# When a gate's product may start: a time for one transposing transfer in the list of an attention and mixture-of-experts kernel

## The chip, the cores and the metric

The kernel runs on one core of one Trainium2 chip. The metric is the device time of one execution in microseconds, the median of several runs. The core's engines are named as the profile names them: PE (TensorE) multiplies, and PEld is its loading of weights; DVE (VectorE) and ACT (ScalarE) work on elements and empty PSUM; POOL (GpSimd) works on elements in SBUF and issues gathers; SP (SyncE) issues nearly all other transfers. Each engine works through its own list of instructions in order, and the lists wait for each other by semaphores.

## The reference

Two stages follow each other. The first is causal attention with a decay, over 8 batches of 8 heads with 576 positions of 64 elements. The second routes every token to one of 8 experts, and each token's expert can depend on the token before it:

```python
decay = cum[:, :, :, None] - cum[:, :, None, :]          # cum: cumsum of log f
scores = np.where(causal, -1e9, scale * q @ k.T + decay)
attn = softmax(scores);  x = attn @ v                    # x: [8, 576, 512]
logits = x @ w_gate                                      # 512 -> 8
local_gate = sigmoid(x @ w_local)
for b, s:  e = argmax(logits[b, s]) if s == 0 or local_gate[b, s] < 0.5 else prev_e
           out[b, s] = softmax(logits[b, s])[e] * (relu(x[b, s] @ w1[e]) @ w2[e])
```

## The kernel before

Attention runs batch by batch, from 0 to 7. A batch is cut into 25 units. A unit has steps on several engines: scores on PE into a PSUM bank `st` (`sc`), a maximum `nm` on DVE (`mx`), the exponential `P` on ACT (`ex`), its transposes on PE into `pt` (`tr`), the high half `ph` on ACT (`hi`), the low half `pl` on DVE (`lo`), and the product with v on PE into `xp` (`av`). Numbers are carried as a high and a low half in 16 bits, so products come in threes. Twenty units treat the 512 first queries of a batch, the last five the 64 last queries, whose result is `xnl`.

Beside its own units a batch carries the preparation of the next one: POOL splits the loaded `ldq`, `ldk` and `ldv` into halves (`t16q`, `t16k`, `VH`, `VL`), PE transposes them into `st`, ACT or DVE copies them out as `Aq` and `Ak`, and SP copies parts of these into `QB` and `KB`. `pump` hands these steps out, some before each unit, from `queue`.

When a batch is done, its result goes the same way: POOL splits `xn` into `xr` and `xnl` into `xl`; SP transposes `xr` in two transfers into `xt` (`turn_x` in `finish_main`) and `xl` in one into `xlt` (`turn_x` in `finish_last`, L781), and writes both to DRAM as `xs`. A batch later, `gate(b)` multiplies them by the gate's weights on PE: its step `mult` (L804) is 32 products of `xt` and 8 of `xlt` into one PSUM bank, `half` and `add` bring the logits together in `L`. Every second gate is followed by the steps of `route`, which find each token's expert and its place; the largest of them is `marks` (L1475), five long instructions, on DVE for the third group of two batches, partly on POOL for the first two.

The order of all these is written by a planner while the kernel is built. It keeps a clock for every engine (`clock`, in modelled nanoseconds), a list of steps for each stage (`line`) and one list, `chain`, for gates and routing. `issue` (L1221) asks `start_of` for each stage and `side_next` (L1184) for the chain when the next step could start, takes the one whose time plus a weight is smallest, and emits it. A chain's step that is possible at once has the weight -700, so it goes first; one that isn't has the weight 0. A gate enters the chain after the unit `GI` of the next batch (unit 21, 14 or 12). `side_next` holds `mult` back until `XD` says that all three transposing transfers of its batch have been emitted (`XD` is 3); for the time it takes those to be done the planner has no number. The seven gates from 0 to 6 go through this chain; that of batch 7 is placed by hand behind attention, as is the whole expert stage, whose first steps begin while attention ends: the gathers `xg` of the first experts' tokens, and the splitting of expert 0's weights on POOL (`stg` into `wh`, `wl`, `uh`, `ul`).

Of the kernel before, what the change touches and what calls it, by code (L numbers as in the profile page):

```python
# [63 lines left out]

T0 = 9700.0
DUE = (("k2", 11000), ("q2", 12500), ("k3", 14500), ("q3", 15500), ("v", 18000), ("v4", 20500), ("a", 26000), ("b", 29000))

NB = (4, 5, 4)
NOV = 31
# [3 lines left out]
def kernel(  # L73
# [208 lines left out]
    def split(hi, lo, t, fast):  # L282
        if fast:
            nc.scalar.copy(hi, t)
            nc.vector.tensor_tensor(lo, t, hi, ALU.subtract)
        else:
            nc.gpsimd.tensor_scalar(hi, t, 1.0, 1.0, ALU.mult, ALU.mult)
            nc.gpsimd.tensor_tensor(lo, t, hi, ALU.subtract)
# [16 lines left out]
    def hi_lo(hi, lo, t, n):  # L305

        m, w = t.shape[1], 1
        for d in t.shape[2:]:
            w *= d
        out = [(m * w, lambda: nc.gpsimd.tensor_scalar(hi, t, 1.0, 1.0, ALU.mult, ALU.mult))]  # L310
        for i in range(0, m, n):
            e = min(i + n, m)
            out.append((2 * (e - i) * w,
                        lambda i=i, e=e: nc.gpsimd.tensor_tensor(lo[:, i:e], t[:, i:e], hi[:, i:e], ALU.subtract)))
        return out
# [421 lines left out]
        clock["DVE"] += 600  # L737


    XT, XD = {}, {}  # L740

    def finish_main(b, xn):
        xr = pools["small"].tile([128, 4, 2, DM], F16, name="xr", bufs=1)
# [30 lines left out]
    def finish_last(b, xnl):  # L774
        xl = pools["small"].tile([128, 2, 4, 64], F16, name="xl", bufs=1)
        xlt = pools["small"].tile([128, 4, 128], F16, name="xlt", bufs=1)
        XT[b].append(xlt)
        t0 = b * S + 512

        def turn_x():  # L780
            nc.sync.dma_start_transpose(out=xlt, in_=xl.rearrange("p a j d -> p (a j d)"))  # L781
            put_xl()
            XD[b] = XD.get(b, 0) + 1

        def put_xl():
            for r in range(2):
                nc.sync.dma_start(out=xs[t0:t0 + 64].rearrange("q (a r e) -> r q a e", a=2, r=2)[r],
                                  in_=xl[r * 64:(r + 1) * 64].rearrange("q a j d -> q a (j d)"))

        if b == B - 1:  # L790
            split(xl[:, 0], xl[:, 1], xnl, True)
            EX["xl"] = xl, xlt
            put_xl()
        else:
            for i, x in enumerate(hi_lo(xl[:, 0], xl[:, 1], xnl, 4) + [(0, turn_x)]):
                queue.insert(min(XI, len(queue)) + i, x)
# [37 lines left out]
    def compute(b, T):  # L834
# [268 lines left out]
        for j in range(4):  # L1103
            d1unit(j)
        d2unit()
        then(-1, lambda: finish_last(b, X["xnl"]))
        lb, lc = (max((i for i in range(20) if i % 5 == x), key=UO.index) for x in (3, 4))
        if b < B - 1:
# [27 lines left out]
    clock = {"PE": T0, "ACT": T0, "DVE": T0, "POOL": T0}  # L1136
# [36 lines left out]
    POOL = 1  # L1173
    OPENS = "mult", "rows", "ends", "carries", "back", "place", "invert", "pinvert", "fill"
    SHUTS = "add", "rows2", "hold", "scan1", "onehot", "place2", "invert2", "pinvert2", "fill2"
    chain = deque()
    side = {"end": (0.0, "PE"), "run": None, "cost": None}
# [6 lines left out]
    def side_next():  # L1184
        eng, cost = COSTS.get(chain[0].__name__, ("DVE", 160))
        after = [side["end"]]
        if chain[0] is early_tok and "open" not in EX or XD.get(getattr(chain[0], "batch", None), 0) < 3 and hasattr(chain[0], "batch"):
            return None, eng, cost
        if chain[0].__name__ in OPENS and side["run"] is None:
            if not room["psS"]:  # L1190
                return None, eng, cost
            after.append(min(room["psS"]))
        now = 0 if side["cost"] is POOL else clock[eng]
        return max([now] + [t + WAIT[src, eng] for t, src in after]), eng, side["cost"] or cost

# [25 lines left out]
    def issue(until=None):  # L1221
        while any(line.values()):
            ready = [(start_of(st), line[st][0][0] + RANK[st], st) for st in STAGES if line[st]]
            if chain:
                ready.append((side_next()[0], serial[0] + RANK["side"], "side"))
                W["side"] = side_weight(*side_next())
            t, _, st = min((x for x in ready if x[0] is not None), key=lambda x: (x[0] + W[x[2]], x[1]))
            if due and due[0][0] <= t and all(room[r] for r in due[0][2]):
                due.popleft()[1]()
                continue  # L1230
            if st == "side":
                side_issue(*side_next())
                continue
            n, u, prev = line[st].popleft()
            eng, cost, fn, takes, frees = u[st]
            for r, c in takes.items():
                for _ in range(c):
                    room[r].remove(min(room[r]))
            fn()
            clock[eng] = t + cost  # L1240
            ends[n, st] = t + cost, eng
            if st == "eq":
                turned[u["key"]] = t + cost
            for r, c in frees.items():
                room[r] += [ends[n, st]] * c
            if (n, st) == until:
                return
# [493 lines left out]
    def open_small():  # L1741
# [7 lines left out]
          "a": due_a, "b": due_b, "nop": nop}  # L1749
    due.extend((T, DO[f], ("psS", "psT") if f in ("k2", "k3", "q2", "q3") else ()) for f, T in DUE)  # L1750

# [515 lines left out]
```

## Time and profile before

| what | value |
|---|---|
| time, median of 3 runs | 856.01 us (855.11 to 859.09) |
| the profiled execution's own time | 858.83 us |
| its span | 857.1 us, 21126 instructions |
| PE busy | 785.4 us, 92% of the span |
| DVE, ACT, POOL busy | 62%, 51%, 48% of the span |
| mean granted clock of PE | 0.976 of full |

The span is what the profiler saw between the first and the last instruction; the execution's own time is 1.7 us more. Attention fills the time from the start to 431 us, the experts the rest.

### The profile page before, as it was taken

The page shows a single profiled execution, that of the slowest core. Times are in us where ns is not written, and L with a number is a line of the kernel's source. Part 1 is how long each engine was busy: PE and PEld are TensorE (multiplying, and loading weights), DVE is VectorE, ACT ScalarE, POOL GpSimd, SP SyncE. Part 2 cuts the span into 40 slices and gives each one's busy share as a digit, 9 for nine tenths or more (in the row PEclk, how much of TensorE's full clock was granted, in tenths as well). Part 3 has the DMA queues.
Part 4 walks back from the last instruction along what each step waited for, and adds up shares of the span by engine and source line. Part 5 has one row for each costly group of instructions (what it writes and reads, how often), then busy time and mean ns, then how long its engine had stood idle before and what let it go on. Part 6 is the DMA issues. An engine that isn't in the chain of part 4 may idle for free. (4 is left out here: it accounts for less than half of the span.)

```text
span 857.1 us, 21126 instructions
## 1 busy us (share of the span) xinstructions
PE 785.4 (92%) x8510; PEld 546.9 (64%) x8510; DVE 529.3 (62%) x1125; ACT 434.4 (51%) x807; POOL 408.9 (48%) x479
## 2 busy tenths in 40 slices
PE   5897999889998799878987899999999999999996
PEld 3676778767877678767753555575564847566543
DVE  8885878898867888798848742443163644525120
ACT  4785878758866688657821413333242423324221
POOL 9598938488753968532976252221311212130201
PEclk9998999999989999998999999999999999999999
DMA  7979768596781859329674641848264553736101
GB/s 167 192 165 193 160 112 168 123 180 144 140 197 42 157 140 158 70 47 229 161 165 185 194 142 50 216 147 203 95 171 149 155 182 121 193 116 185 51 0 47
DMA packets 196517, 122.46 MB, mean 143 GB/s; under 512 B 136220, under 2 KB 172318, under 8 KB 196396
## 3 DMA queue, kind: packets, MB, share of 16 engines
q1 hardware_dynamic: 190273, 101.68, 51.6%
q0 software_dynamic: 6144, 19.41, 7.0%
q8 instruction: 68, 1.11, 0.5%
q14 instruction: 32, 0.26, 0.1%
HBM read 72.41 MB, written 19.62 MB: 107 GB/s over the span
## 5 line engine op out<-in xcount | busy, mean ns | idle before, releaser
L1690 PE MATMUL z<-xT,wh 128*128 128x288 f16 (+4 forms) x960 | 182.3, 301 | 3.8 <-DVE hl L1671 3.8
L899 ACT ACTIVATE P<-st,nm 128x512 f32<-128x512 f32 (+3 forms) x288 | 152.4, 584 | 38.5 <-DVE nm L879 35.3
L879 DVE TENSOR_REDUCE nm<-st 128x1 f32<-128x512 f32 (+4 forms) x264 | 134.1, 542 | 23.2 <-PE st L875 16.8
L1671 DVE SCALAR_TENSOR_TENSOR hl<-z,hh 128x576 f16<-128x576 f32 (+5 forms) x80 | 53.0, 662 | 154.0 <-ACT hh L1670 153.8
L919 ACT CAST ph<-pt 128x512 f16<-128x512 f32 (+1 forms) x200 | 115.8, 583 | 50.1 <-PE pt L914 48.6
L914 PE MATMUL pt<-ident,P 128*128 128x128 f32 x784 | 124.7, 283 | 13.0 <-DVE pl L923 8.0
L923 DVE TENSOR_TENSOR pl<-pt,ph 128x512 f16<-128x512 f32 x168 | 111.6, 668 | 26.3 <-ACT ph L919 24.0
L1690 PEld LDWEIGHTS <-wh 128*128 128x128 f16 x960 | 93.2, 98 | 43.7 <-issue 4.9
L1690 PE MATMUL z<-xT,wl 128*128 128x288 f16 (+4 forms) x480 | 118.4, 301 | 0.0
L1712 PE MATMUL y<-uh,hh 128*128 128x512 f16 x288 | 109.9, 381 | 1.6 <-ACT o L1680 1.6
L1712 PE MATMUL y<-uh,hl 128*128 128x512 f16 x288 | 109.9, 382 | 0.0
L1712 PE MATMUL y<-ul,hh 128*128 128x512 f16 x288 | 109.7, 381 | 0.0
L1670 ACT ACTIVATE hh<-z 128x576 f16<-128x576 f32 (+5 forms) x80 | 46.0, 575 | 121.1 <-PE z L1690 121.0
L914 PEld LDWEIGHTS pt<-ident,P 128*128 128x128 f32 x784 | 85.8, 144 | 28.9 <-issue 7.5
L1712 PEld LDWEIGHTS <-hh 128*128 128x128 f16 x576 | 56.5, 98 | 70.4 <-issue 6.2
L1682 POOL DMA_INDIRECT out_dram<-o,ranki x26 | 27.3, 1051 | 149.0 <-ACT o L1680 115.8
L893 PE MATMUL xp<-VH,pl 128*128 128x65 f16 (+1 forms) x960 | 92.3, 195 | 4.3 <-DVE pl L923 4.3
L893 PE MATMUL xp<-VH,ph 128*128 128x65 f16 (+1 forms) x960 | 94.3, 198 | 0.9 <-ACT ph L919 0.9
L893 PE MATMUL xp<-VL,ph 128*128 128x65 f16 (+1 forms) x960 | 93.2, 196 | 0.0
L893 PEld LDWEIGHTS <-ph 128*128 128x128 f16 (+1 forms) x1920 | 85.0, 103 | 7.7 <-issue 2.5
L868 PE MATMUL st<-KB,QB 70*128 70x256 f16 (+4 forms) x448 | 80.1, 287 | 8.5 <-DMA KB<-Ak 7.1
L868 PE MATMUL st<-Ak,Aq 128*128 128x256 f16 (+4 forms) x448 | 80.7, 291 | 7.3 <-ACT P L899 7.1
(390 smaller groups left out, 1316.3 us busy)
## 6 DMA issues: line engine op xcount, KB each, us to landing
stg<-in_moe_w_dram SPq DMA_DIRECT2D x64, 512.0 KB
xs<-xr SPq DMA_DIRECT2D x16, 512.0 KB
ldq<-in_q_dram SPq DMA_DIRECT2D x14, 512.0 KB
ldk<-in_k_dram SPq DMA_DIRECT2D x14, 512.0 KB
ldv<-in_v_dram SPq DMA_DIRECT2D x28, 256.0 KB
QB<-Aq SPq DMA_DIRECT2D x15, 256.0 KB
KB<-Ak SPq DMA_DIRECT2D x15, 256.0 KB
ldv<-in_v_dram SPq DMA_DIRECT2D x20, 64.0 KB
```

Of the source, the lines that this page charges most:

```text
L868: nc.tensor.matmul(st[p0:p0 + m, co:co + n], lhsT=queries(lq, kk, h, c), rhs=rhs, start=(ps == 0 and first and co == col), stop=(ps == 1), ...
L879: nc.vector.tensor_reduce(dst, src, axis=AX.X, op=ALU.max, negate=True)
L893: nc.tensor.matmul(xo, lhsT=a[:, c0:c0 + m], rhs=w[:, vi, :], start=False, stop=(i == n - 1 and jj == 2), skip_group_check=True)
L899: nc.scalar.activation(P[:, c0:c1].rearrange("p (k x r) -> p k r x", r=2, x=64), st[:, c0:c1].rearrange("p (k r x) -> p k r x", r=2, x=64) ...
L914: nc.tensor.matmul(U["pt"][:, i * 128:(i + 1) * 128], lhsT=P[:, i * 128:(i + 1) * 128], rhs=ident, is_transpose=True, start=(i == 0), stop ...
L919: nc.scalar.copy(U["ph"][:, :cols], U["pt"][:, :cols])
L923: nc.vector.tensor_tensor(U["pl"][:, :cols], U["pt"][:, :cols], U["ph"][:, :cols], ALU.subtract)
L1670: nc.scalar.activation(hv, z[:, 0:nh, 0:wd], AF.Relu)
L1671: nc.vector.scalar_tensor_tensor(lv, z[:, 0:nh, 0:wd], 0.0, hv, ALU.max, ALU.subtract)
L1682: nc.gpsimd.indirect_dma_start(out=outf, out_offset=bass.IndirectOffsetOnAxis(ap=scat(t), axis=0), in_=o, in_offset=None, bounds_check=NT ...
L1690: nc.tensor.matmul(z[:, a, 0:wd], lhsT=w[:, d, fc * 128:(fc + 1) * 128], rhs=xT[:, x, a * wd:(a + 1) * wd], start=(i == 0), stop=(i == len ...
L1712: nc.tensor.matmul(y, lhsT=a[:, fc, t * 128:(t + 1) * 128], rhs=u[:, fc], start=(i == 0), stop=(i == len(prods) - 1))
```

## The change

A number `XL` is added, and `finish_last` notes, when it emits the transposing transfer of a batch's `xl`, a time `XR`: the later of POOL's and PE's modelled clocks at that moment plus 4500 modelled nanoseconds. `side_next` then lets no gate's first step start in the plan before that time. The emitted instructions are the same in kind and number on each engine; their order is not.

```diff
 DUE = (("k2", 11000), ("q2", 12500), ...
+XL = 4500
...
-    XT, XD = {}, {}
+    XT, XD, XR = {}, {}, {}
...
             nc.sync.dma_start_transpose(out=xlt, in_=xl.rearrange("p a j d -> p (a j d)"))
             put_xl()
             XD[b] = XD.get(b, 0) + 1
+            XR[b] = max(clock["POOL"], clock["PE"]) + XL
...
             after.append(min(room["psS"]))
+        if hasattr(chain[0], "batch") and side["run"] is None:
+            after.append((XR[chain[0].batch], "PE"))
         now = 0 if side["cost"] is POOL else clock[eng]
```

Lines behind the change are up to four further down in the new kernel: L816 is L818 there, L868 is L870, L781 is L782, L1479 is L1483.

All five lists are the same up to gate 3, so gates 0, 1 and 2 stand where they stood. On PE, gate 3 follows the products with v at once in the kernel before:

```order
5760 L893 MATMUL xp<-VL_126,ph 128x65
5761 L893 LDWEIGHTS pl
5762 L893 MATMUL xp<-VH_124,pl 128x65
5763 L816 LDWEIGHTS xt
5764 L816 MATMUL st<-wg,xt 128x18
```

In the new kernel attention's own work follows there:

```order
5761 L895 LDWEIGHTS pl
5762 L895 MATMUL xp<-VH_124,pl 128x65
5763 L870 LDWEIGHTS Aq
5764 L870 MATMUL st<-Ak,Aq 128x512
5765 L870 LDWEIGHTS QB_120
5766 L870 MATMUL st<-KB_122,QB_120 128x512
5767 L877 LDWEIGHTS mA
5768 L877 MATMUL st<-mB,mA 128x128
5769 L916 MATMUL pt<-ident,P 128x128 x4
```

and gate 3 begins in row 5928 (100 matmuls further down):

```order
5925 L895 MATMUL xp<-VL_126,ph 128x65
5926 L895 LDWEIGHTS pl
5927 L895 MATMUL xp<-VH_124,pl 128x65
5928 L818 LDWEIGHTS xt
5929 L818 MATMUL st<-wg,xt 128x18
```

So only gate 3 itself is moved back in this place. Behind it, everything that the planner decides comes out otherwise: gate 4 begins in row 7130 (row 7192 before), gate 5 in row 8335 (row 8374 before), gate 6 in row 9514 (row 9492 before). On SP, the transposing transfer for gate 5 stood behind the copies into `QB_121` and the parts of `KB_123`:

```order
162 L351 DMA QB_121<-augt 3x512
163 L757 DMA xs<-xr 64x4x1024 x2
164 L378 DMA QB_121<-Aq 64x2x1024 x2
165 L382 DMA QB_121<-Aq 64x512
166 L339 DMA KB_123<-augm 3x4096
167 L351 DMA KB_123<-augt 3x512
168 L781 DMA_TRANSPOSE xlt<-xl 128x4x128
```

and now stands ahead of them:

```order
161 L352 DMA QB_121<-augt 3x512
162 L758 DMA xs<-xr 64x4x1024
163 L782 DMA_TRANSPOSE xlt<-xl 128x4x128
164 L789 DMA xs<-xl 128x1x256 x2
165 L758 DMA xs<-xr 64x4x1024
166 L379 DMA QB_121<-Aq 64x2x1024 x2
167 L383 DMA QB_121<-Aq 64x512
```

The transfer for gate 5 no longer waits in SP's list for those copies. The steps of `route` move too. On DVE, the five instructions of the third `marks` (from `HI` to `LO`) followed each other without a step of attention between them, just as batch 7 begins:

```order
592 L1473 TENSOR_TENSOR hm<-t_192,ov 128x10
593 L1479 TENSOR_TENSOR HI<-imain,hm 128x480
594 L1483 TENSOR_SCALAR RH<-HI,irow 128x10x48
595 L1485 TENSOR_SCALAR RH<-HI,irow 128x2x48
596 L1490 TENSOR_TENSOR RH<-HI,icol 128x10x48
597 L1491 TENSOR_TENSOR LO<-i_176,lo 128x1280
598 L879 TENSOR_REDUCE nm<-st 128x1 x5
```

and now stand among low halves `pl` of batch 6's last units:

```order
590 L1483 TENSOR_TENSOR HI<-imain,hm 128x480
591 L925 TENSOR_TENSOR pl<-pt,ph 128x512
592 L1487 TENSOR_SCALAR RH<-HI,irow 128x10x48
593 L925 TENSOR_TENSOR pl<-pt,ph 128x512
594 L1489 TENSOR_SCALAR RH<-HI,irow 128x2x48
595 L925 TENSOR_TENSOR pl<-pt,ph 128x256
596 L1494 TENSOR_TENSOR RH<-HI,icol 128x10x48
597 L1495 TENSOR_TENSOR LO<-i_176,lo 128x1280
598 L956 RECIPROCAL rs<-xp 128x4
599 L881 TENSOR_REDUCE nm<-st 128x1
```

Only the last two of the five stand side by side now, and the third `marks` comes before batch 6's last units are done, no longer after. Two smaller moves go with these. The second `marks`, in batch 5, begins in row 441 on DVE (row 422 before). And on POOL the first three quarters of the splitting of expert 0's first weights (`stg`, `wh`, half of `wl`) stand ahead of the six gathers `xg` instead of behind them.

## Rows read from the trace of the kernel before

**Rows 1.** The page: busy time by engine, granted clock in 40 slices.
```profile
PE 785.4 (92%) x8510; PEld 546.9 (64%) x8510; DVE 529.3 (62%) x1125; ACT 434.4 (51%) x807; POOL 408.9 (48%) x479
PEclk9998999999989999998999999999999999999999
```
**Rows 2.** Waits of PE, whole span: us in total, times, longest.
```profile
PE st L868 <- ACT P L899: 7.1, 6, 4.7
PE st L816 <- DMA xlt<-xl: 4.4, 2, 2.4
```
**Rows 3.** Timeline of PE at gate 3: start, us, instruction, idle time before.
```profile
243.86 0.95 PE L816 MATMUL st<-wg,xt 128*128 128x18 f16 x32
246.74 0.59 PE L816 MATMUL st<-wg,xlt 128*64 128x18 f16 x8 [1.94 <-DMA xlt<-xl]
247.27 1.12 PE L914 MATMUL pt<-ident,P 128*128 128x128 f32 x4
```
**Rows 4.** Timeline of PE at gate 5.
```profile
347.88 0.95 PE L816 MATMUL st<-wg,xt 128*128 128x18 f16 x32
351.26 0.42 PE L816 MATMUL st<-wg,xlt 128*64 128x18 f16 x8 [2.42 <-DMA xlt<-xl]
352.11 0.65 PE L914 MATMUL pt<-ident,P 128*128 128x128 f32 x4
```
**Rows 5.** Timeline of SP at gates 3, 4 and 5.
```profile
243.77 1.83 SPq L781 DMA_TRANSPOSE xlt<-xl  x1
...
282.32 2.29 SPq L781 DMA_TRANSPOSE xlt<-xl  x1
...
348.76 1.23 SPq L781 DMA_TRANSPOSE xlt<-xl  x1
```
**Rows 6.** Timeline of POOL: the split that gate 3's transfer waits for.
```profile
237.41 0.67 POOL L314 TENSOR_TENSOR xl<-xnl,xl 128x256 f16<-128x256 f32 x1
```
**Rows 7.** Line L816 at gate 4: count, duration ns, first and last start.
```profile
L816 PE MATMUL st<-wg,xlt x8: 177/177/198, 309.4 to 309.7; 128*64 128x18 f16 x8
```
**Rows 8.** Windows behind both waits: engines' busy time, instructions, clock, DMA, GB/s.
```profile
246.70:253.50 6.80, 6.76 (x42) 5.35 (x43) 3.34 (x11) 2.65 (x6) 0.58 (x2) 0.50 0.90 219
352.30:355.90 3.60, 3.60 (x30) 2.61 (x29) 2.99 (x10) 1.61 (x4) 3.35 (x6) 0.53 0.02 5
```
**Rows 9.** Line L974, once per batch: first and last mark used here.
```profile
L974 PE MATMUL st<-mB,mA x4: 193/193/203, 106.6 to 106.7; 128*128 128x64 f16 x4
...
L974 PE MATMUL st<-mB,mA x4: 193/193/203, 360.7 to 360.8; 128*128 128x64 f16 x4
```
**Rows 10.** Windows from mark to mark, batches with gates 1, 3 and 5.
```profile
106.60:152.30 45.70, 43.80 (x752) 36.59 (x746) 37.17 (x90) 36.95 (x78) 27.01 (x27) 1.00 0.74 148
206.90:256.40 49.50, 47.38 (x740) 38.82 (x739) 38.07 (x90) 37.35 (x77) 31.63 (x32) 0.93 0.73 154
311.70:360.70 49.00, 46.02 (x747) 37.65 (x739) 38.56 (x93) 37.69 (x77) 33.64 (x35) 0.97 0.60 113
```
**Rows 11.** Window ahead of gate 3.
```profile
203.60:243.80 40.20, 40.02 (x688) 32.99 (x685) 32.91 (x74) 33.05 (x67) 30.96 (x32) 1.00 0.72 147
```
**Rows 12.** Timeline of DVE: first and last of the third marks' five.
```profile
380.89 1.46 DVE L1479 TENSOR_TENSOR HI<-imain,hm 128x480 f16<-128x480 f16 x1
...
385.05 1.48 DVE L1491 TENSOR_TENSOR LO<-i,lo 128x1280 f16<-128x1280 f16 x1
```
**Rows 13.** Timeline of PE there.
```profile
387.92 0.59 PE L868 MATMUL st<-Ak,Aq 128*128 128x512 f16 x1 [4.66 <-ACT P L899]
```
**Rows 14.** Window behind it.
```profile
386.80:393.30 6.50, 5.38 (x29) 3.87 (x28) 4.43 (x11) 4.52 (x10) 0.00 (x0) 0.50 1.08 256
```
**Rows 15.** Timeline of POOL: first gather, last low half of expert 0's first weights.
```profile
395.26 1.24 POOL L1643 DMA_INDIRECT xg<-xs,xg  x1 [10.74 <-DVE pl L923]
...
424.52 2.27 POOL L314 TENSOR_TENSOR wl<-stg,wh 128x512 f16<-128x512 f32 x2
```
**Rows 16.** Timeline of PE: the first expert's first products.
```profile
431.16 0.50 PE L1690 MATMUL z<-xT,wh 128*128 128x384 f16 x2
```

## The prediction

> **What bounds the kernel now.** I read the page first. PE is busy 92% of the span, the next engine 62% [rows 1], so what PE stands idle for is what can be won, and the row of the granted clock shows a second thing to win: it is not at full level everywhere [rows 1]. Next came PE's waits, longest in total first. Among them one belongs to the change: the gate's products wait for the transfer into `xlt` twice, 4.4 us in all [rows 2]. The timeline shows where. At gate 3 the 32 products of `xt` are done by 244.8 us and the first of `xlt` starts at 246.74, 1.94 us of idle time before it [rows 3]. At gate 5 it is the same with 2.42 us, up to 351.26 [rows 4]. The other gates from 0 to 6 do not wait for it: the wait's count is two, and both are seen.
>
> The windows behind the waits show that PE loses more than the idle time. From 246.7 to 253.5 the granted clock is 0.50, so 1.2 instead of 2.4 GHz, and PE is busy 6.76 of these 6.8 us; from 352.3 to 355.9 it is 0.53 with PE busy throughout [rows 8]. Ahead of gate 3 the clock was 1.00 for 40.2 us with PE busy 40.02 of them [rows 11], so the fall follows the wait. Four transposes take 1.12 us at the lower level and 0.65 at the higher [rows 3, 4].
>
> **Why the transfers come late.** POOL finishes the split of `xl` for gate 3 at 238.1 [rows 6], but SP issues the transfer only at 243.77 [rows 5], after the copies and parts that stand ahead of it in its list. PE comes to the gate at 243.86 [rows 3]: issue and use coincide, and the data is there 2.9 us after the issue (246.7 less 243.8). Gate 5 has 348.76 and 347.88 [rows 4, 5]. Gate 4's transfer, which stands ahead of those copies, is issued at 282.32 [rows 5] and first used at 309.4 [rows 7], with no wait.
>
> **The change, part by part.**
>
> *The new time itself.* It adds no instruction and no wait on the chip; it moves rows in the lists. Up to gate 3 nothing moves, so some 244 us are as before.
>
> *Gate 3* goes behind 100 further matmuls. Ahead of the gate PE did 688 in 40.2 us [rows 11], 58 ns each, so it reaches the gate 5.8 us later, at 249.7, and `xlt` after 0.95 us of `xt` products, at 250.6. The data landed at 246.7, and the lists of SP and POOL up to its transfer are the same, so the margin is 3.9 us. The wait goes, and what stands in its place is attention's scores, which read the same `Aq`, `Ak`, `QB` and `KB` as the scores just before. What is late next there is nothing that the trace shows, as the margin is larger than the wait.
>
> *Gate 5* comes 20 matmuls earlier, 1.2 us, but its transfer goes to the place in SP's list that gate 4's transfer had in the kernel before: in front of the copies. Gate 4's was issued 27 us ahead of use [rows 5, 7], so this wait goes as well. What is queued behind the transfer on SP are the copies into `QB_121` and `KB_123`; they need data that POOL splits after `xl`, so they lose about the transfer's 1.23 us of issuing [rows 5] and no more. They are needed when batch 7 begins, some 20 us later.
>
> *Gates 4 and 6* move by 31 matmuls forward and 11 back, 1.8 and 0.6 us at 58 ns. Gate 4 keeps over 20 of its 27 us. Both cost nothing.
>
> *What the two waits are worth.* The first bound is the idle time alone, 1.94 + 2.42 = 4.4 us. The second adds half of PE's busy time at the lower level, 3.4 + 1.8, and makes 9.6; but PE would then run into the other engines sooner. Between the bounds lies a measurement that the trace holds. Line L974 runs once per batch; its six times used here are 106.6, 152.3, 206.9, 256.4, 311.7 and 360.7 [rows 9], and from one to the next in batches with the gates 1, 3 and 5 the work is nearly the same, 740 to 752 matmuls. Gate 1 does not wait and its stretch takes 45.7 us at a clock of 1.00; the stretches of gates 3 and 5 take 49.5 and 49.0 [rows 10]. So a wait with all that follows costs 3.8 and 3.3 us, and I take their sum, 7.1 us, for both.
>
> The Trainium skill (TensorE: Matmul & The Clock Gate, Terms) puts the penalty of a throttled stretch at its length times the missing share of the clock. By it the two stretches would cost 6.8 x 0.50 + 3.6 x 0.47 = 5.1 us, an estimate, and with the idle time 9.5 us. The rows from mark to mark show less, 7.1, and they decide; by the page's sum the time would be 846.5.
>
> *Routing.* Its steps move on DVE and POOL without a change in number. In the second group `marks` comes later, in the third it comes earlier and mixed with low halves. DVE's work in the stretch is the same, so I put this at zero, as for any exchange of places in a list. The bounds: the five instructions of the third `marks` now hold DVE from 380.89 to 386.5 [rows 12], PE stands idle 4.66 us before 387.92 [rows 13] and then works 5.38 of 6.5 us at a clock of 0.50 [rows 14]. If all this goes, 4.66 + 5.38 / 2 = 7.4 us are won; if two new pauses of that kind arise, 14.7 us are lost. The nearest rows for an ordinary new pause are those of the gates, 3.3 to 3.8 us each.
>
> *The start of the experts.* Some 3.3 us of splitting stand ahead of the gathers now. The first gather starts at 395.26, POOL having been idle for 10.74 us [rows 15], so this fills a pause, if the weights have landed. Expert 0's last low half is done at 426.8 (424.52 + 2.27) [rows 15], and PE, which starts with the first quarter of these weights at 431.16 [rows 16], needs the last after more than a microsecond: a margin of over 5 us. All of it shifts forward with attention, so the gain stays. If the cover were gone, what exceeds the margin would be lost one for one.
>
> **The sum.** The profiled execution took 858.83 us, its span 857.1 and 1.7 around it. 858.83 - 7.1 = 851.7. The median of the runs shown is 856.01, 2.8 us less than this execution; the same 7.1 us off the median gives 848.9, so I predict 849.0. What a measurement can tell from no change is about 0.5%, 4.3 us, so below 851.7 is faster and above 860.3 slower.
>
> **The rivals.**
>
> *More is won.* The pause at 383 us goes too, since only two of the five instructions stand side by side now. For it: the mixed order lets PE have low halves between them. Against: DVE is the engine that is full there, and the same work mixed in among batch 6's last units can hold those up. If half or all of the 7.4 us go, the time is 841.5 to 845.3; I take 843.5. Chance 0.14.
>
> *The gain is partly turned into a new wait.* Elsewhere in batches 4 to 7 the new order makes PE pause once more for 2 us or so, with the lower clock behind it; the place could be the second `marks`, at whose `HI` and `LO` DVE and POOL wait for each other. For it: PE waits for ACT's `P` in six cases, up to 4.7 us [rows 2], so such pauses do arise where lists meet. Against: the margins of the moved rows. One such pause costs 3.3 to 3.8 [rows 10], and the time is about 852.5: within 0.5%. Chance 0.24, with the case in it that the change does not do what it says, because one gate still waits; the margins of 3.9 us and more speak against that.
>
> *Slower.* The third `marks` stands before the end of batch 6's units now. Each of its five instructions, 5.6 us together [rows 12], holds up the low half behind it, that one the products with v, and as `pt` has only two banks, the next transposes. If PE pauses at each for as long as it takes, it loses 5.6 us, and as the pauses repeat, the clock stays at the lower level until batch 7's scores run: three stretches like the one behind the old pause, each with 5.38 / 2 = 2.7 us lost [rows 14], make 8.1. That is 849.0 + 5.6 + 8.1 = 862.7. It decides where pauses and lower clock together exceed 7.1 + 4.3 = 11.4 us. For it: five low halves that PE needs stand behind or between them now. Against it: the old pause, 7.4 us by the same count, would have to stay beside it, though it is made by the same five instructions. Chance 0.06.
>
> **How the numbers follow.** The forecast, 849.0, has a chance of 0.56, with a range of its own from 846.4 (both waits at the upper bound of 9.6) to 851.6 (the idle time alone). Faster by more than 0.5%: 0.56 + 0.14 = 0.70. Within 0.5%: 0.24. Slower: 0.06. The range for eight times in ten goes from 843.5, the value taken for the larger gain, to 855.5, where two ordinary pauses (3.3 each) use up nearly all of the gain; what is left out on both sides is the larger gain's far half and the slower case with a part of the middle one.
>
> **What would show it.** Right: PE's waits have no row for `xlt` at the gates 3 and 5; the granted clock is 1.00 in the 10 us behind both; the stretches of L974 around gates 3 and 5 take about 46 us; attention's end, which the first expert products mark, moves from 431.2 to about 424. Wrong: if the waits are gone and the stretches stay at 49 us, then the other engines set the pace there, and the step from idle PE to time fails; if attention's end moves by 7 us and the kernel's does not, the experts' start has eaten it; if the clock falls in places where it did not before, the new order has its own pauses.

## The result, and the profile after

The change makes the kernel faster by a little under one per cent: 849.16 us in the median of six runs (848.63 to 852.49) against 856.55 (853.96 to 859.31, six runs), ratio 0.9917, 95% interval 0.989 to 0.9945. The forecast was 849.0. The profiled execution took 849.11 us, its span 847.4. The number is right for a reason that is only half the one that I gave: more was won in attention than I forecast, and more was lost behind it, so that it came out is in part luck.

The page of the kernel after, in the two lines that answer to [rows 1]:

```profile
PE 781.5 (92%) x8510; PEld 545.0 (64%) x8510; DVE 518.0 (61%) x1125; ACT 433.9 (51%) x807; POOL 408.9 (48%) x479
...
PEclk9798999999999999999989999999999999999998
```

The work is the same, instruction for instruction. PE's waits in the whole span (total, times, longest), as in [rows 2]:

```profile
PE psG L818 <- DMA xt<-xr: 6.5, 2, 4.8
...
PE st L870 <- ACT P L901: 3.2, 5, 1.7
```

There is no row for `xlt` any more, and the waits for `P` have halved. In their place stands a wait of gate 7 (`psG`, the last gate) for `xt`, 6.5 us. It had 0.6 us in the kernel before:

```profile
PE psG L816 <- DMA xt<-xr: 0.6, 1, 0.6
```

First the places of the change, PE at the gates 3 and 5 [rows 3, 4]:

```profile
250.10 0.95 PE L818 MATMUL st<-wg,xt 128*128 128x18 f16 x32
250.98 0.42 PE L818 MATMUL st<-wg,xlt 128*64 128x18 f16 x8
...
337.29 0.95 PE L818 MATMUL st<-wg,xt 128*128 128x18 f16 x32
338.17 0.42 PE L818 MATMUL st<-wg,xlt 128*64 128x18 f16 x8
```

and SP, which issues the transfers of the gates 3, 4 and 5 [rows 5]:

```profile
242.79 1.77 SPq L782 DMA_TRANSPOSE xlt<-xl  x1
...
280.95 2.70 SPq L782 DMA_TRANSPOSE xlt<-xl  x1
...
331.03 2.71 SPq L782 DMA_TRANSPOSE xlt<-xl  x1
```

From issue to use it is 8.2 and 7.1 us at the gates 3 and 5, and neither product has idle time before it. The windows behind both (us, PE, PEld, DVE, ACT, POOL busy, granted clock, DMA, GB/s), as in [rows 8], have the clock at 1.00 where it was 0.50 and 0.53:

```profile
250.90:258.00 7.10, 7.10 (x119) 5.07 (x116) 6.29 (x22) 6.29 (x16) 1.42 (x3) 1.00 0.87 193
338.20:345.00 6.80, 6.80 (x96) 5.67 (x94) 6.47 (x19) 5.44 (x13) 6.47 (x9) 1.00 0.63 140
```

From mark to mark (L974, now L976), batches with the gates 1, 3 and 5 [rows 10]:

```profile
105.60:151.30 45.70, 43.80 (x750) 36.55 (x747) 37.25 (x90) 36.99 (x78) 27.14 (x29) 1.00 0.74 151
...
205.90:252.70 46.80, 46.62 (x788) 38.81 (x787) 38.62 (x90) 39.94 (x83) 33.57 (x34) 1.00 0.72 148
...
302.90:353.70 50.80, 49.45 (x833) 41.22 (x832) 44.13 (x110) 42.13 (x86) 38.25 (x42) 1.00 0.60 107
```

The marks no longer enclose the same work: there are 788 and 833 matmuls where there were 740 and 747. At the 58 ns per matmul of [rows 11] the two stretches would be 44.0 and 45.8 us with the old counts, 5.5 and 3.2 less than before.

Attention's end, by the first expert product (414.19 against 431.16 in [rows 16]), then two short waits for the first expert's weights, and gate 7 behind them, on PE:

```profile
414.19 0.50 PE L1694 MATMUL z<-xT,wh 128*128 128x384 f16 x2
...
416.14 0.50 PE L1694 MATMUL z<-xT,wh 128*128 128x384 f16 x2 [0.31 <-POOL wh L311]
417.43 0.34 PE L1694 MATMUL z<-xT,wl 128*128 128x384 f16 x1 [0.78 <-POOL wl L315]
...
429.77 0.58 PE L818 MATMUL psG<-wg,xt 128*128 128x18 f16 x16 [4.84 <-DMA xt<-xr]
432.04 0.60 PE L818 MATMUL psG<-wg,xt 128*128 128x18 f16 x16 [1.69 <-DMA xt<-xr]
```

POOL, which answers to [rows 15]: its first work on the experts' weights, the first gather, the first of the second three, and the first step of the split of `xr` that gate 7 waits for.

```profile
385.76 1.05 POOL L1621 TENSOR_SCALAR stg<-stg 128x1024 f32<-128x1024 f32 x1 [9.78 <-PE st L877]
...
389.36 1.24 POOL L1647 DMA_INDIRECT xg<-xs,xg  x1 [0.18 <-issue]
...
399.40 0.96 POOL L1647 DMA_INDIRECT xg<-xs,xg  x1 [6.27 <-DMA xT<-xg]
...
421.95 1.05 POOL L288 TENSOR_SCALAR xr<-xn 128x1024 f16<-128x1024 f32 x1
```

The same split in the kernel before:

```profile
430.77 1.04 POOL L287 TENSOR_SCALAR xr<-xn 128x1024 f16<-128x1024 f32 x1
```

Attention ends 17.0 us earlier. POOL begins its work for the experts 9.5 us earlier (385.76, now with weights, against 395.26 with the gathers), and `xr` is split 8.8 us earlier. So PE now arrives before POOL. To see where each microsecond went I divided the profiled executions at three instructions: the first mark [rows 9], the first expert product, and the start of the last product of gate 7. In us:

| kernel | to first mark | to first expert product | to gate 7's last product | to the span's end | span |
|---|---|---|---|---|---|
| before | 106.6 | 324.6 | 11.5 | 414.4 | 857.1 |
| after | 105.6 | 308.6 | 18.8 | 414.4 | 847.4 |
| held | 106.6 | 315.2 | 11.6 | 413.3 | 846.7 |
| g5only | 105.7 | 317.8 | 10.3 | 411.2 | 845.0 |
| a_fast | 105.6 | 313.1 | 10.2 | 413.0 | 841.9 |
| b_fast | 107.1 | 329.8 | 10.7 | 410.0 | 857.6 |
| gap5 | 106.6 | 308.6 | 14.1 | 413.1 | 842.4 |
| held_gap5 | 106.7 | 317.6 | 10.6 | 409.3 | 844.2 |
| xl3 | 108.3 | 317.5 | 10.3 | 409.0 | 845.1 |
| xl7 | 107.2 | 308.4 | 13.0 | 414.9 | 843.5 |
| xl7_gap5 | 104.9 | 309.8 | 10.3 | 417.3 | 842.3 |

After against before: 1.0 less ahead of the first mark, where the lists are the same (chance), 16.0 less in attention, 7.3 more up to gate 7, nothing behind it: 9.7 in all. Of the 7.3, 5.9 are the longer wait for `xt` and 1.1 the two waits for weights.

### The profile page after: what moved, and what is told of

Its sections match the earlier page's. It is cut to its first block, busy times and chain, and to the rows that moved or that the text cites. A ratio compares the mean times of both kernels' runs of the same rounds, so it can differ in the third digit from the quotient of the medians.

```text
span 847.4 us, 21119 instructions
## 1 busy us (share of the span) xinstructions
PE 781.5 (92%) x8510; PEld 545.0 (64%) x8510; DVE 518.0 (61%) x1125; ACT 433.9 (51%) x807; POOL 408.9 (48%) x479
## 4 chain that ended last, share of the span: by engine, by line
PE 60%; issue 10%; DVE 9%; DMA 7%; POOL 6%; ACT 4%; SPq 1%; POOLq 1%; ACTq 0%; DVEq 0%
PE z L1694 16%; PE y L1716 15%; PE st L870 8%; PE pt L916 7%; PE xp L895 6%; PE st L458 2%; DVE pl L925 2%; DMA KB<-Ak 2%; DMA xT<-xg 1%; ACT P L901 1%; DVE nm L881 1%; PE st L877 1%; POOLq L1685 1%; POOL wl L315 1%; DMA xt<-xr 1%
## 5 line engine op out<-in xcount | busy, mean ns | idle before, releaser
L881 DVE TENSOR_REDUCE nm<-st 128x1 f32<-128x512 f32 (+4 forms) x264 | 134.6, 543 | 15.3 <-PE st L877 11.6
L916 PE MATMUL pt<-ident,P 128*128 128x128 f32 x784 | 122.1, 280 | 13.1 <-DVE pl L925 9.6
L870 PE MATMUL st<-KB,QB 70*128 70x256 f16 (+4 forms) x448 | 79.6, 287 | 6.8 <-DMA KB<-Ak 6.8
L870 PE MATMUL st<-Ak,Aq 128*128 128x256 f16 (+4 forms) x448 | 80.0, 290 | 3.4 <-ACT P L901 3.2
```

The lines of the kernel that those rows point to most:

```text
L870: nc.tensor.matmul(st[p0:p0 + m, co:co + n], lhsT=queries(lq, kk, h, c), rhs=rhs, start=(ps == 0 and first and co == col), stop=(ps == 1), ...
L881: nc.vector.tensor_reduce(dst, src, axis=AX.X, op=ALU.max, negate=True)
L916: nc.tensor.matmul(U["pt"][:, i * 128:(i + 1) * 128], lhsT=P[:, i * 128:(i + 1) * 128], rhs=ident, is_transpose=True, start=(i == 0), stop ...
```

## The experiments

The theory: the two waits are worth some 7 to 9 us; the new plan from gate 3 on wins as much again in attention; POOL's list at the start of the experts eats that second part. The rivals: the waits are worth little by themselves and the new order won it all; or the start of the experts is set by something other than POOL.

**held: the transfers earlier, no other engine's list touched.** SP's copies that stood ahead of the two transfers are kept until these are issued:

```diff
+                if nm == "q" and b in (5, 7) and XD.get(b - 2, 0) < 3:
+                    HELD.setdefault(b - 2, []).append(f)
+                else:
+                    f()
...
             XD[b] = XD.get(b, 0) + 1
+            free(b)
```

> The kernel before with one edit in SP's list alone: the copies into QB of batches 5 and 7 and the parts that follow k wait until the transfers into xlt of gates 3 and 5 have been issued, so these transfers go out ahead of them. The lists of PE, DVE, ACT and POOL are word for word those of the kernel before. Theory A (the two waits are worth 7.1 us by themselves, and the rest of the gain at attention's end is from the new places of the routing): PE has no wait for xlt at gates 3 and 5, the clock behind them is 1.00, the first expert product moves from 431.2 to about 424, gate 7's wait for xt stays about 0.6 us and the time falls by about 7, to 849. Theory B (the waits are the pace of other engines showing, and the gain came from the new order alone): the waits go but other pauses take their place, the stretches around gates 3 and 5 stay at 49 us and the time stays within 2 us of the kernel before.

Measured: 849.5 us (847.35 to 853.9), ratio 0.9908 (0.9877 to 0.9938), 7.9 us less than the 857.7 of before beside it (5.3 to 10.5). SP in this kernel:

```profile
238.01 2.28 SPq L796 DMA_TRANSPOSE xlt<-xl  x1
...
336.66 2.57 SPq L796 DMA_TRANSPOSE xlt<-xl  x1
```

The transfers go out 5.8 and 12.1 us earlier than in [rows 5]; gate 3's right behind POOL's split of `xl`, which ends at 238.0 in this execution. The stretches of the gates 3 and 5:

```profile
206.80:251.10 44.30, 44.12 (x742) 36.60 (x738) 37.76 (x91) 37.15 (x77) 30.67 (x31) 1.00 0.73 150
...
305.40:351.00 45.60, 44.30 (x745) 36.67 (x740) 38.97 (x93) 37.43 (x77) 34.65 (x36) 1.00 0.65 122
```

With the same matmuls as before they take 44.3 and 45.6 us, not 49.5 and 49.0: 5.2 and 3.4, together 8.6. The first expert product is 9.4 us earlier, and gate 7's wait is 0.6 us as before. Theory A holds, with a larger value than its 7; theory B falls. This kernel, without the change's new plan, is as fast as the change.

**a_fast and b_fast: gate 7's `xr` without POOL.** Two of the last batch's splits move to ACT and DVE, in the kernel after (a_fast) and before (b_fast):

```diff
-            return [lambda: part(0, 2, False, 1), lambda: part(2, 1, False, 0), lambda: part(3, 1, True, 3)]
+            return [lambda: part(0, 2, True, 1), lambda: part(2, 1, True, 0), lambda: part(3, 1, True, 3)]
```

> The changed kernel with two of the last batch's splits of xr moved from POOL to ACT and DVE; all lists ahead of attention's end are as in the changed kernel. Theory A (POOL at the experts' start eats the rest of what attention won: gate 7 waits 6.5 us for xt because xr's split stands behind weights on POOL, with a low clock behind it): that wait falls below 1.5 us and the time falls by 5 to 6 us, to about 844. Theory B (the experts' start waits for something else too, the gathers or the weights on POOL, which is late next): gate 7's wait goes, but the wait moves to the low or high halves of the weights, and the time stays within 1.5 us of the changed kernel's 849.

> The same edit of the last batch's splits on the kernel before. Theory A (there gate 7 waits only 0.6 us, since attention ends later and POOL has the time): the time stays within 1 us of the kernel before, 856. Theory B (the splits on ACT and DVE are better whatever attention does): 4 to 6 us faster here as well, and then the loss at the experts' start does not come from attention's earlier end.

Measured: a_fast 844.31 us (843.05 to 847.22), ratio 0.9845 (0.9819 to 0.9871); b_fast 858.65 (855.98 to 862.11), ratio 1.0015 (0.9996 to 1.0034). Gate 7 in a_fast (count, duration in ns, first and last start):

```profile
L818 PE MATMUL psG<-wg,xt x32: 170/170/173, 427.8 to 428.6; 128*128 128x18 f16 x32
```

Its 32 products run without a wait, and the part up to gate 7 shrinks from 18.8 us to 10.2. The edit has a price in attention, where DVE's splits now stand ahead of work that PE waits for:

```profile
413.16 1.07 PE L916 MATMUL pt<-ident,P 128*128 128x128 f32 x4 [4.91 <-DVE rs L956]
```

That costs 4.5 us there (5.2 in b_fast), and a_fast is still some 5 us faster than the change. Since PE arrives 4.5 us later, not all of the 8.6 us come from the faster split: gate 7's last product starts 4.1 us earlier than in the change. On the kernel before the same edit changes the median by 1 us, inside its interval, and the part up to gate 7 shrinks only by 0.8 us, against 8.6. So the loss up to gate 7 belongs to POOL's `xr` and to attention's earlier end, as theory A has it. The unchanged time of b_fast is not a sign that nothing moved there: in the table, 5.2 us more in attention stand against 4.4 less behind gate 7, which the last section takes up.

**g5only, g5again, g5third: gate 5 alone is held back.** Three profiles of one kernel, here against the kernel after:

```diff
-        if hasattr(chain[0], "batch") and side["run"] is None:
+        if getattr(chain[0], "batch", None) == 5 and side["run"] is None:
             after.append((XR[chain[0].batch], "PE"))
```

> The kernel before with gate 5 alone held further back; gate 3 stays where it was, with its wait. Theory A (each wait has its own price, and the new places of the routing behind gate 5 remove the pause at 383 us): gate 3's wait and its stretch of 49.5 us stay, gate 5's wait goes (3.3 us), the last stretch up to attention's end is 4 to 5 us shorter, attention ends 7 to 8 us earlier than before, and as the experts' start has only about a microsecond of cover for xr, 2 to 3 us of it are lost there: time about 850 to 852. Theory B (the gain in the last batch hangs on the place of gate 3, by the new routing of the first groups): attention's end moves by 3.3 us alone and the time is about 853.

> The kernel with gate 5 alone held back, word for word as in the run g5only, once more with a profile. There the 2.0 us wait at gate 3 was followed by a clock of 1.00 and its stretch took 46.4 us, and this execution (846.77) was 6 us below the median of its runs. Theory A (whether the clock falls behind the 2-us wait is decided anew in each execution, and the fall costs about 3 us more): where this profile shows 0.50 behind gate 3, its stretch takes 49 to 50 us and the time is 850 to 854; where it shows 1.00, 46 to 47 us. Theory B (the clock is not it): the stretch and the clock behind gate 3 don't go together.

> As g5again, a third profile of the same kernel, for the same question: stretch of gate 3 of 49 to 50 us where the clock behind its wait is 0.50, and 46 to 47 us where it is 1.00 (Theory A); no such pairing (Theory B).

Measured: 852.96 us (846.77 to 854.0), ratio 0.9941 (0.9915 to 0.9966), and 850.0 and 850.87 in the two single runs. The last stretch between marks is 53.4 us (354.0 to 407.4), as before (53.3), so nothing is won there: theory B is nearer, with 4.7 us by the medians (2.9 to 7.3). It is not that the pause of 4.66 us stayed. PE's longest wait for `P` is 0.8 us in g5only, but new pauses stand in its place, the two longest of them these:

```profile
386.05 0.18 PE L885 MATMUL xp<-eps 1*128 1x6 bf16 x1 [2.28 <-DVE xn L960]
...
391.13 0.20 PE L895 MATMUL xp<-VH,pl 128*128 128x65 f16 x1 [2.47 <-DVE pl L925]
```

What the three profiles show of gate 3, which still waits here, is worth more. First g5only, the timeline of PE at gate 3's product:

```profile
246.16 0.42 PE L818 MATMUL st<-wg,xlt 128*64 128x18 f16 x8 [2.00 <-DMA xlt<-xl]
```

and its stretch from mark to mark:

```profile
206.20:252.60 46.40, 44.21 (x744) 36.63 (x738) 37.78 (x91) 37.38 (x77) 30.70 (x31) 1.00 0.70 146
```

g5again, the product:

```profile
245.79 0.42 PE L818 MATMUL st<-wg,xlt 128*64 128x18 f16 x8 [1.93 <-DMA xlt<-xl]
```

and the stretch:

```profile
205.90:252.30 46.40, 44.28 (x746) 36.67 (x740) 37.84 (x91) 37.49 (x77) 30.73 (x31) 1.00 0.70 145
```

g5third, the product:

```profile
247.00 0.60 PE L818 MATMUL st<-wg,xlt 128*64 128x18 f16 x8 [2.30 <-DMA xlt<-xl]
```

and the stretch:

```profile
206.80:256.40 49.60, 47.12 (x740) 38.60 (x739) 38.07 (x90) 37.36 (x77) 31.35 (x32) 0.93 0.75 157
```

The wait is 1.9 to 2.3 us in all. Where the clock stays at 1.00 the stretch takes 46.4 us, where it falls 49.6. Beside the 44.3 of held this parts the price of gate 3's wait: 2.1 us for the idle time, 3.2 for the lower clock. Theory A on the clock holds for the stretch. It does not explain the whole spread of the times: g5again kept its clock at gate 3 and still took 850.0.

**gap5 and held_gap5: POOL's pause between the gathers is filled.** The second three gathers go behind five pieces of weight work:

```diff
-        for e in range(2):
+        def tok(e):
             xT = EX["xT", e] = ep.tile([128, 8, 128 * EARLY], F16, name=f"xT{e}")
             tokens(ep, xT, lambda i: EX["g"][:, CAP * e + i:CAP * e + i + 1], EARLY, (B - 2) * S)
+        tok(0), queue.insert(min(len(queue), 5), (0, lambda: tok(1)))
```

> The changed kernel with the second three gathers of POOL moved behind five pieces of weight work, which fill the 6.27 us in which POOL waits for the transposes of the first three; nothing else moves on PE, DVE or ACT. Theory A (POOL's list sets the experts' start: gate 7 waits for xr's split because POOL is late, and it is late because it stands idle between its gathers): POOL works 4.7 us of the pause, xr's split ends some 4.5 us earlier, about 422.5 instead of 427, gate 7's wait falls from 6.5 to about 1 to 2 us, attention's end stays at 414.2, and the time falls by 5 to 7 us to 842 to 844. Theory B (the weights or their loads are late next, or the second gathers are needed at once): POOL's pause moves to a later place, gate 7's wait stays above 4 us and the time stays within 2 us of 849.

> The same edit of the gathers in the kernel with SP's list alone changed (the run held). There gate 7 waits only 0.6 us for xt. Theory A (POOL's pause counts only where gate 7 has to wait): the time stays within 1.5 us of that run, 848 to 850. Theory B (the gathers' place is worth something by itself): it falls by 4 us or more.

Measured: gap5 844.78 us (843.13 to 846.53), ratio 0.9848 (0.9813 to 0.9883). The timeline of POOL at the second gathers:

```profile
400.48 1.05 POOL L1647 DMA_INDIRECT xg<-xs,xg  x1 [1.63 <-DMA xT<-xg]
```

and of PE at gate 7:

```profile
426.21 0.56 PE L818 MATMUL psG<-wg,xt 128*128 128x18 f16 x16 [1.75 <-DMA xt<-xr]
428.43 0.59 PE L818 MATMUL psG<-wg,xt 128*128 128x18 f16 x16 [1.66 <-DMA xt<-xr]
```

POOL's pause of 6.27 us is 1.63, attention's part is the same 308.6 us, gate 7 waits 3.4 us instead of 6.5, and the time falls by some 4 to 6 us (4.4 by the medians, 5.9 by the ratios). The wait was put at 1 to 2 us and the time at 842 to 844, so the sizes were missed; the direction is theory A's. held_gap5 took 846.86 us (845.98 to 849.28), 2.6 less than held: between both theories. Gate 7 had nothing to win there; the table has 2.4 us more in attention, 1.0 less up to gate 7 and 4.0 less behind it. The last section has a likely reason for the last of these.

**xl3, xl7, xl7_gap5: other distances.** 3000 and 7000 in place of 4500, the latter also with gap5's edit:

```diff
-XL = 4500
+XL = 3000
```

> The changed kernel with 3000 in place of 4500 as the distance behind the transfer that the gate keeps; gate 3 stands about 27 matmuls further ahead and the plan behind it comes out otherwise. Theory A (the two waits are worth 8 to 9 us at attention's end, and the further 6.6 us of the changed kernel there are a property of that one plan): the waits for xlt are gone here too, the first expert product lies anywhere from 414 to 424, and the time lies between 845 and 851. Theory B (the distance itself matters): a wait for xlt of 0.5 us or more comes back at gate 3 or 5, with a lower clock behind it, and the time is 851 to 855.

> The changed kernel with 7000 in place of 4500; gate 3 stands some 26 matmuls further back and the plan behind it comes out otherwise again. Theory A as for 3000: no wait for xlt, first expert product from 414 to 424, time from 845 to 851. Theory B (a gate that stands further back makes its routing late and holds up the batch behind it): attention's end is later than 424 and the time 851 to 857.

> The two best edits together: the distance of 7000 and the second gathers behind five pieces of weight work. In the run with 7000 alone gate 7 waited 2.4 us and POOL stood idle 5.77 us between its gathers. Theory A (POOL is the pace there): xr's split ends 4 to 5 us earlier, gate 7's wait goes, and the time falls by 3 to 5 us from 845.4, to 840.5 to 842.5. Theory B (next is SP's list, in which xt's transposes stand behind those of the gathers, or the weights' loads): the wait stays above 1.5 us and the time stays within 1.5 us of 845.4.

Measured: xl3 847.06 us (ratio 0.9875, 0.983 to 0.9919), xl7 845.4 (0.9849, 0.9805 to 0.9893), xl7_gap5 847.29 (0.9869, 0.9849 to 0.989). No wait for `xlt` at the gates 3 and 5 in any of them. Attention's part takes 317.5 us with 3000 and 308.4 with 7000, so what the change wins there beyond its waits does not come with every distance; whether it hangs on the distance or on the plan that happens to follow, three distances do not tell. With 3000 the first expert product starts at 425.8, later than the 414 to 424 expected, and the time is within its range. xl7_gap5 missed its expectation. Gate 7's wait is gone, but behind gate 7 it takes 417.3 us where xl7 takes 414.9, with this among PE's waits:

```profile
PE psG L1501 <- DVE LOl L1495: 3.5, 1, 3.5
```

At least a part of it is DVE: three of the steps ahead of `LOl` take 0.89, 1.12 and 1.02 us while POOL splits weights up to 449.3, and 0.17, 0.35 and 0.25 in xl7, where POOL has ended by 450.0, before they start. The profiled execution (843.99) is 3.3 us below the median of its runs, though, so the profile does not show all that this median lost, and the intervals of xl7 and xl7_gap5 overlap. The fastest kernels are a_fast, gap5 and xl7, within 1.1 us of each other; a_fast's interval lies wholly below that of the change.

## Why the prediction was right, and where it was wrong

**The gates: right.** Both waits are gone, both clocks are at 1.00, and nothing that was passed on SP or moved on PE is late there. Gate 3 is reached at 250.1 us, forecast 249.7. Further on only the sizes differ: gate 4's first product starts at 295.2 us, 14 us behind its transfer and not over 20, which costs nothing.

**"What the two waits are worth": the term was too small.** I took 7.1 us, from the stretch of gate 1 as the one without a wait. held shows 8.6 in the two stretches and 9.4 at attention's end. For gate 5 the yardstick of 45.7 us was right (45.6 in held, 3.4 us instead of 3.3). For gate 3 it was wrong (44.3, 5.2 instead of 3.8): gate 1's stretch has 1.9 us of idle PE of its own [rows 10] (45.70 less 43.80), gate 3's without its wait only 0.2 (44.30 less 44.12). Similar counts do not make two stretches alike. The sum that I set aside, 9.5 by the Trainium skill (TensorE: Matmul & The Clock Gate, Terms), comes closer to the 9.4; held's interval of 5.3 to 10.5 us in the times admits both.

**"Routing", put at zero: wrong.** Against held, which has the waits removed and the old plan, the change's attention is 6.6 us shorter (308.6 against 315.2). The windows from the first mark to the first expert product show that 6.2 of them are idle time of PE (28.5 us in held, 22.3 in the change, span of the window less PE's busy time). First held:

```profile
106.60:421.84 315.24, 286.77 (x4745) 233.32 (x4739) 266.92 (x631) 236.72 (x485) 207.95 (x224) 0.99 0.68 141
```

and the change:

```profile
105.60:414.19 308.59, 286.31 (x4741) 234.22 (x4739) 261.88 (x631) 236.58 (x485) 200.20 (x221) 0.98 0.68 142
```

The pause of 4.66 us ahead of 387.92 [rows 13] is gone, as in the rival *more is won*; two waits of 1.7 us are left around the third `marks`, with the clock at 0.56 from 366 to 369 us. But g5only and xl3 lack that pause too, and their attention is no shorter than that of held (317.8 and 317.5 us), so its absence is not enough.

My reason for the zero was that DVE's work is the same. The instructions are, their time is not: DVE is busy 5.0 us less in the same windows. The five of the third `marks` took 5.7 us before (two of them in [rows 12]), beside POOL's split of `xr`. On DVE:

```profile
382.39 1.12 DVE L1483 TENSOR_SCALAR RH<-HI,irow 128x480 f16<-128x480 f16 x1
```

and on POOL:

```profile
381.93 2.59 POOL L314 TENSOR_TENSOR xr<-xn,xr 128x512 f16<-128x512 f32 x2
```

In the change they take 3.35 us, and POOL's last work ahead of them has ended at 362.9. On DVE:

```profile
364.03 0.65 DVE L1483 TENSOR_TENSOR HI<-imain,hm 128x480 f16<-128x480 f16 x1
365.20 0.33 DVE L1487 TENSOR_SCALAR RH<-HI,irow 128x480 f16<-128x480 f16 x1
```

and on POOL:

```profile
360.67 2.27 POOL L315 TENSOR_TENSOR xr<-xn,xr 128x512 f16<-128x512 f32 x2
```

Over the profiles the two go together: the five take 3.35 to 3.8 us in the change, gap5, xl7 and xl7_gap5, whose attention takes 308.4 to 309.8 us, and 5.2 to 6.1 us, beside a working POOL, in held, held_gap5, xl3 and g5only, where it takes 315.2 to 317.8. (The kernel before and b_fast have both waits beside it, and a_fast its own price in attention.) That is a pairing; no run keeps POOL away from these five steps and changes nothing else, so the cause of the 6.6 us stays open.

**"The start of the experts": the step that failed.** I checked one consumer of POOL, the first expert's weights, found over 5 us of margin and wrote that all of it shifts forward, so the gain stays. Two things were wrong with it. POOL does not shift with attention: it began its work for the experts 9.5 us earlier while attention's end came 17.0 earlier. That used up the margin that I had found, and PE waits 1.1 us for the first expert's weights. And a second consumer with no margin stands in the same list: gate 7 waited 0.6 us for `xr` already. The wait became 6.5 us, the clock behind it is 0.53 (429.7 to 436.9 us), and the part up to gate 7 grew by 7.3. The prediction had named this sign ("the experts' start has eaten it"), but as what would prove it wrong, without a price.

**Why the number came out.** In us against before: 9.4 for the waits instead of 7.1, 6.6 more for the routing instead of 0, 7.3 given back instead of 0, and 1.0 of chance. More was won than the waits, as in the rival *more is won*, and a new wait took it back, though not in batches 4 to 7, where the rival *turned into a new wait* had it, but at gate 7. That the two nearly cancel is luck. On the medians the change is worth what held alone is worth.

## What to carry to other kernels

When a stage is made to end earlier, look through the queue of every engine that feeds the next stage, and for each consumer ask how late it is already: a wait of 0.6 us in the trace of before is a margin of zero, and all that is won ahead of it may stop there. Price a wait by an edit that removes nothing else, or by the same stretch with and without it; another stretch with a similar count may have idle time of its own. And when a small change makes a planner lay out everything anew, run the wait's removal without the new plan, since both effects come in one number.

## What the runs showed of the hardware

**The same wait, two clocks.** Ahead of gate 3 PE waited 1.94 us [rows 3], 2.14 (b_fast) and 2.30 (g5third) in three profiles, and the clock behind the wait was 0.50 to 0.54. It waited 2.00 (g5only) and 1.93 (g5again) in two others with the same lists up to there, and the clock stayed at 1.00. The length of the wait does not part the two cases, and what decides it these rows do not tell. At gate 3 it is worth about 3.2 us: the stretch takes 49.5, 49.3 and 49.6 us where the clock fell, and 46.4 twice where it did not.

**DVE's small steps beside POOL's.** The chain of routing behind gate 7 runs on DVE, and its steps take several times as long while POOL works through weights. In the kernel before, the timeline of DVE:

```profile
457.38 1.29 DVE L1443 TENSOR_TENSOR_SCAN IN<-carry,OHA 128x80 f16<-128x80 f16 x1
458.71 0.97 DVE L1445 TENSOR_TENSOR EX<-IN,OHA 128x80 f16<-128x80 f16 x1
```

and that of POOL beside it:

```profile
457.34 2.28 POOL L314 TENSOR_TENSOR wl<-stg,wh 128x512 f16<-128x512 f32 x2
459.70 1.04 POOL L1617 TENSOR_SCALAR stg<-stg 128x1024 f32<-128x1024 f32 x1
```

In held_gap5, where POOL ends its weights at 450.22 and rests to 459.86, first DVE:

```profile
450.35 0.33 DVE L1459 TENSOR_TENSOR_SCAN IN<-carry,OHA 128x80 f16<-128x80 f16 x1
450.70 0.20 DVE L1461 TENSOR_TENSOR EX<-IN,OHA 128x80 f16<-128x80 f16 x1
```

and POOL:

```profile
447.95 2.27 POOL L314 TENSOR_TENSOR wl<-stg,wh 128x512 f16<-128x512 f32 x2
459.86 1.05 POOL L1659 DMA_INDIRECT xg<-xs,mg  x1 [9.65 <-DVE tot L1959]
```

The scan takes 0.33 us instead of 1.29, the step behind it 0.20 instead of 0.97. The Trainium skill (SBUF — State Buffer, Who interferes with whom) states that a DVE instruction with two inputs in SBUF and a GpSimd instruction that reads SBUF contend, and that the later one blocks until the other is done. These rows agree to within 0.2 us: the slow scan starts 0.04 us behind POOL's first instruction, which ends near 458.5 (half of 2.28 further on), and the scan is done at 458.7. The step into `RH` of the third `marks`, shown above, reads one tensor only, and it is slower beside POOL as well. Slow steps fit the 4.0 us that held_gap5 wins behind gate 7 against held. Of the eleven kernels in the table, three have this scan at 0.33 us, b_fast, held_gap5 and xl3, and they are the three that are shortest behind gate 7 (409.0 to 410.0 us, the others 411.2 to 417.3). No run here isolates it, though: POOL's lateness at the start of the experts may then be paid twice, at gate 7 and in the routing behind it.
